# Attention and two expert layers on one core: a gather awaited on the load queue, more buffers for row statistics, and a new order of steps

## The chip, the cores and the metric

The kernel runs on one core of a Trainium2 chip. The metric is the device time of one execution in microseconds, as the median of several runs. The engines have short names in the profile: PE is TensorE (its matmuls; PEld is its loading of weights), DVE is VectorE, ACT is ScalarE, POOL is GpSimd, SP is SyncE, which here only issues transfers. Each engine carries out its own instructions in the order in which they are written, and waits for the others by semaphores.

## The reference

Three layers follow one another. The first is causal attention with 2 batches, 12 heads, 448 tokens and 64 columns a head:

```python
scores = scale * np.matmul(q, k.transpose(0, 1, 3, 2))      # scale = 1/8
scores = np.where(mask, -1000000000.0, scores)
scores = scores - np.max(scores, axis=-1, keepdims=True)
attn = np.exp(scores)
attn = attn / (np.sum(attn, axis=-1, keepdims=True) + 1e-09)
return np.matmul(attn, v).astype(np.float32)
```

Its output, 896 tokens of 768 columns, goes to a layer of 8 experts in which each token takes the expert with the largest logit (a cosine of token and expert embedding, over tau), `h = relu(x @ w1[e])`, `out = gate * (h @ w2[e])` with 1024 hidden columns and the softmax probability as the gate. Third, `h = max(max(x @ w1, x @ w2), x @ w3)` and `h @ w_out`, all 768 by 768, whose weights come in float64 and are decoded on the chip.

## The kernel before, in words

**Pairs.** Attention works on twelve pairs of heads, 0 to 9, a and b (hexadecimal); pairs 0 to 5 are batch 0, pairs 6 to b batch 1. The scores of a pair are cut into seven blocks of 64 queries (i = 0 to 6, with 64(i+1) keys), in four groups: {6}, {5, 0}, {4, 1}, {3, 2}. The order in which all this is issued is written out by hand in the strings of `SCHEDULE`, one word a step; `emit` reads the words one after the other, so a word's place is its place in the queue of each engine on which it works. A word begins with the pair; the next letter is the step:

- `L`, `V`: loads of K and Q, and of V, issued by SP. `q`: K times 1/8, by GpSimd (`2qp`), VectorE (`0qv`) or ScalarE (`6qs`), one instruction on 128x448.
- `S`, `Z`: TensorE's scores of a group's first and second block (a letter behind names the PSUM tag); `K`: the mask, added by a matmul.
- `M`: row maxima (VectorE); `E`: exponentials with row sums (ScalarE); `R`: reciprocal (VectorE). All three use the pair's tile `sm` (`sms[p]`), from a pool of two buffers.
- `N`: one block of `prb` is multiplied by the reciprocal, by VectorE, or with a `p` by GpSimd. `prb` has two buffers, for even and odd pairs.
- `T`: four transposes of `prb` (TensorE), `t`: their copy to `pt` by ScalarE (`s`) or VectorE (`v`). `T0` reads blocks 0 to 3, `T1` blocks 2 and 4 to 6, `T2` blocks 3 to 6, `T3` blocks 4 to 6.
- `A`: the product with V; `a`: its copy to `xt`. `X`: four transposes of `xt`, `x`: their copy to `x2T`, after which GpSimd stores the pair's columns into the DRAM tensor `xd`.

**Beside attention.** Words with `D` decode two weight units of the third layer early (`D10x` loads, `a`, none and `l` are stages). `EA`, `EM`, `ET` prepare the expert embeddings, whose rows lie in the tile `er`. `GA` to `G5` make the logits, `C0` and `C1` choose an expert for each token of a batch. `F1`, `F2`, `F3` (a chain of small VectorE instructions between matmuls) find the most frequent expert of batch 0 and up to 128 of its tokens. With that, slot 0 of the expert layer begins before attention is done: `L0` loads its four w1 tiles, `L1`, `L11` and `L13` its four w2 tiles (768 KB each, on SP; six buffers `raw` in turn), `W` words split them into a high part (ScalarE, `h`) and a low part (VectorE, `l`), `XG` gathers the 128 tokens from `xd` into `xrp` (an indirect transfer issued by GpSimd that must wait for the six stores of batch 0), `X0` and `X4` transpose them, and `H` words are its first layer.

**After attention.** The last string orders the routing of all tokens and slot 0's second layer (`P`, `Y`); then come up to 14 further slots of 128 tokens, and the third layer.

The functions that the diff touches, and what calls them:

Of the kernel before, what the change touches and what calls it, by code (L numbers as in the profile page):

```python
# [7 lines left out]
F32 = mybir.dt.float32  # L8
# [28 lines left out]
def kernel(  # L37
# [45 lines left out]
    xd = dram.tile([N, DM], F32, name="xd")  # L83

# [44 lines left out]
    def embed(tp):  # L129
        er = tp.tile([E, DM], F32, name="er")  # L130
        nc.scalar.dma_start(out=er, in_=emb)
        nc.scalar.dma_start(out=rtau, in_=tau.to_broadcast([P, 1]))
        sq = hp0[:E, :DM]
        es = tp.tile([E, 2], F32, name="es")
        table = tp.tile([E, 2], F32, name="table")
        nc.vector.memset(table, 1.0)
        nc.scalar.activation(out=table[:, 1:2], in_=table[:, 0:1], func=AF.Sqrt)
        return er, es, sq, table
# [282 lines left out]
    sm_p = att.enter_context(tc.tile_pool(name="sm", bufs=2))  # L421
# [297 lines left out]
    def reuse():  # L719
# [11 lines left out]
        "L0": lambda: wload0(0, (0, 1, 2, 3)), "L1": lambda: wload0(1, (0, 2)), "L11": lambda: wload0(1, (1,)), "L13": lambda: wload0(1, (3,)), "RE": reuse, "R0": lambda: held["S0"].relu(0),  # L731
# [429 lines left out]
```

## Time and profile before

| what | us |
|---|---|
| median of 3 runs | 474.25 |
| lowest and highest | 473.67, 474.72 |
| the profiled execution | 473.55 |
| its span in the profile | 471.8 |
| TensorE busy in it | 457.7 |
| VectorE busy | 323.2 |
| ScalarE busy | 266.9 |
| GpSimd busy | 81.0 |

The span is what the profiler saw from the program's first instruction to its last. Attention fills it up to about 106 us; from there to 300 us run the expert slots, then the third layer. A busy time is the union of an engine's instructions; waits inside it show only when the engine is looked at in order of time.

### The profile page before, as it was taken

What the parts mean: (1) busy time and instruction counts of PE and PEld (TensorE: products, weight loads), DVE (VectorE), ACT (ScalarE), POOL (GpSimd) and SP (SyncE); (2) the same over time, 40 slices, a digit from 0 to 9 for tenths busy, and PEclk for the clock granted to TensorE, in tenths of its full rate; (3) what the DMA queues carried; (4) which work ended last, traced back from release to release, by engine and by line L of the source; (5) the groups of instructions that cost most, each with busy time, mean ns of one, the idle gap of its engine ahead of it and who ended that gap; (6) DMA issues with size and microseconds to landing.
All of it is one profiled execution on the core that took longest, in us unless ns stands there. A gap on an engine that the chain in (4) does not pass through costs nothing. (4 is left out here: it accounts for less than half of the span.)

```text
span 471.8 us, 9239 instructions
## 1 busy us (share of the span) xinstructions
PE 457.7 (97%) x3158; PEld 405.8 (86%) x3158; DVE 323.2 (69%) x650; ACT 266.9 (57%) x560; POOL 81.0 (17%) x103
## 2 busy tenths in 40 slices
PE   8999999899999999999999999999999999999994
PEld 6787768688898998998999987989989989899993
DVE  5999999968454985110978955898989889840000
ACT  7898979867726896233988954544444353410000
POOL 4868474620010000000000000000000000001111
PEclk9999999999999999999999999999999999999998
DMA  8644229441158890119799903844534330000111
GB/s 272 251 124 163 65 76 408 183 130 51 34 171 320 309 354 21 35 38 350 279 320 370 365 24 131 343 141 142 180 140 144 125 135 1 1 0 35 67 68 67
DMA packets 18173, 75.85 MB, mean 161 GB/s; under 512 B 2360, under 2 KB 5432, under 8 KB 18112
## 3 DMA queue, kind: packets, MB, share of 16 engines
q1 hardware_dynamic: 15408, 65.05, 38.1%
q0 software_dynamic: 2400, 9.83, 5.6%
q8 instruction: 26, 0.43, 0.4%
q10 hardware_dynamic: 304, 0.25, 0.2%
q14 instruction: 35, 0.29, 0.2%
HBM read 69.62 MB, written 5.51 MB: 159 GB/s over the span
## 5 line engine op out<-in xcount | busy, mean ns | idle before, releaser
L975 PE MATMUL pm<-x2h,dwh 128*128 128x512 f32 (+1 forms) x204 | 74.1, 363 | 0.0
L976 PE MATMUL pm<-x2l,dwh 128*128 128x512 f32 (+1 forms) x204 | 74.0, 362 | 0.0
L977 PE MATMUL pm<-x2h,dwl 128*128 128x512 f32 (+1 forms) x204 | 74.0, 362 | 0.0
L981 PE MATMUL l<-w2h,hh 128*128 128x384 f32 x160 | 54.9, 343 | 0.7 <-ACT hh L207 0.7
L242 DVE TENSOR_TENSOR w1l<-raw,w1h 128x768 fp32r<-128x768 f32 x40 | 36.0, 950 | 27.8 <-PE l L981 20.5
L981 PE MATMUL l<-w2l,hh 128*128 128x384 f32 x160 | 53.7, 336 | 0.2 <-DVE w2l L262 0.2
L981 PE MATMUL l<-w1h,xhp 128*128 128x512 f32 x109 | 43.8, 402 | 0.0
L981 PE MATMUL l<-w1l,xhp 128*128 128x512 f32 x109 | 42.7, 391 | 0.0
L174 ACT CAST dwh<-dt_t 128x768 fp32r<-128x768 f32 (+1 forms) x20 | 15.5, 773 | 46.8 <-DVE dt_t L173 46.7
L977 PEld LDWEIGHTS pm<-x2h,dwl 128*128 128x128 f32 x204 | 38.3, 188 | 4.0
L975 PEld LDWEIGHTS pm<-x2h,dwh 128*128 128x128 f32 x204 | 38.3, 188 | 4.0
L976 PEld LDWEIGHTS pm<-x2l,dwh 128*128 128x128 f32 x204 | 38.3, 188 | 4.0
L517 ACT ACTIVATE prb<-pss,sm 128x64 f32<-128x64 f32 (+6 forms) x84 | 39.2, 492 | 3.3 <-DVE sm L510 2.2
L1115 POOL DMA_INDIRECT out_dram<-ob,sidx x7 | 6.9, 979 | 194.8 <-DVE ob L1114 194.8
L527 POOL TENSOR_SCALAR prb<-prb,sm 128x64 f32<-128x64 f32 (+6 forms) x38 | 36.0, 964 | 19.8 <-DVE sm L523 18.7
L198 POOL DMA_INDIRECT xrp<-xd,idx x11 | 11.3, 1029 | 153.0 <-PE xtp L216 143.1
L981 PE MATMUL l<-w2h,hl 128*128 128x384 f32 x160 | 36.3, 336 | 0.1
L242 DVE TENSOR_TENSOR w2l<-raw,w2h 128x768 fp32r<-128x768 f32 x40 | 35.1, 947 | 0.0
L204 DVE TENSOR_TENSOR hl<-htp,hh 128x512 fp32r<-128x512 f32 x17 | 11.7, 689 | 31.8 <-ACTq L351 17.8
L510 DVE TENSOR_REDUCE sm<-pss 128x1 f32<-128x128 f32 (+6 forms) x84 | 29.9, 412 | 2.9 <-PE pss L506 2.4
L241 ACT CAST w1h<-raw 128x768 fp32r<-128x768 f32 x40 | 31.7, 854 | 0.0
L981 PEld LDWEIGHTS l<-w2h,hh 128*128 128x128 f32 x160 | 30.0, 188 | 1.5 <-ACT hh L207 0.9
(255 smaller groups left out, 1022.4 us busy)
## 6 DMA issues: line engine op xcount, KB each, us to landing
raw<-in_moe_w_dram SPq DMA_DIRECT2D x48, 768.0 KB, 6.5
rawd<-in_moe_w_dram SPq DMA_DIRECT2D x18, 768.0 KB, 5.9
rawd<-in_moe_w_out_dram SPq DMA_DIRECT2D x6, 768.0 KB, 4.3
vr<-in_v_dram SPq DMA_DIRECT2D x12, 256.0 KB, 3.7
kt<-in_k_dram SPq DMA_DIRECT2D x12, 224.0 KB, 4.1
xd<-x2T POOLq DMA_DIRECT2D x12, 224.0 KB, 3.2
qt<-in_q_dram SPq DMA_DIRECT2D x11, 224.0 KB, 3.5
qt<-in_q_dram ACTq DMA_DIRECT2D x1, 224.0 KB
```

The costliest lines, as they stand in the source:

```text
L174: nc.scalar.copy(out=hi[:, c0:c1], in_=f)
L198: nc.gpsimd.indirect_dma_start(out=xrp, out_offset=None, in_=xd if i else xd[0:S], in_offset=bass.IndirectOffsetOnAxis(ap=idx[:, i:i + 1] ...
L204: nc.vector.tensor_tensor(out=lo, in0=ps_ap, in1=hi, op=ALU.subtract)
L241: nc.scalar.copy(out=hi[:, sl], in_=r[:, sl])
L242: nc.vector.tensor_tensor(out=lo[:, sl], in0=r[:, sl], in1=hi[:, sl], op=ALU.subtract)
L510: nc.vector.tensor_reduce(out=sms[p][:, 0, SC[i]:SC[i] + 1], in_=held["s", p, g][:, SO[i]:SO[i] + 64 * (i + 1)], axis=AX.X, op=ALU.max, ne ...
L517: nc.scalar.activation(out=prb[p % 2][:, poff[i]:poff[i] + n], in_=ps[:, SO[i]:SO[i] + n], func=AF.Exp, bias=sm[:, 0, SC[i]:SC[i] + 1], sc ...
L527: eng.tensor_scalar(out=r, in0=r, scalar1=sms[p][:, 2, SC[i]:SC[i] + 1], scalar2=None, op0=ALU.mult)
L975: nc.tensor.matmul(o, lhsT=lh, rhs=rh, start=first, stop=False)
L976: nc.tensor.matmul(o, lhsT=lh, rhs=rl, start=False, stop=False)
L977: nc.tensor.matmul(o, lhsT=ll, rhs=rh, start=False, stop=last)
L981: nc.tensor.matmul(o, lhsT=a, rhs=b, start=first and n == 0, stop=last and n == len(ops) - 1)
```

## The change

Four things are changed. The strings of `SCHEDULE` are written in a new order, with some steps on another engine: K's scaling leaves GpSimd (12 pairs: 9 by GpSimd and 3 by VectorE before, 8 by VectorE and 4 by ScalarE now), GpSimd has 43 normalisations where it had 38, and VectorE 41 for 46. A new word `LW`, ahead of `L1`, `L11` and `L13`, stores one number of `xrp` into a DRAM tensor `mark`, from SP's queue. The pool of `sm` has four buffers. The tile `er` is the first rows of `xrp`.

```diff
@@
+    mark = dram.tile([1, 1], F32, name="mark")
@@ def embed(tp):
-        er = tp.tile([E, DM], F32, name="er")
+        er = xrp[:E]
@@
-    sm_p = att.enter_context(tc.tile_pool(name="sm", bufs=2))
+    sm_p = att.enter_context(tc.tile_pool(name="sm", bufs=4))
@@ once = {
-        "L0": lambda: wload0(0, (0, 1, 2, 3)), "L1": lambda: wload0(1, (0, 2)), ...
+        "L0": lambda: wload0(0, (0, 1, 2, 3)), "LW": lambda: nc.sync.dma_start(out=mark, in_=xrp[0:1, 0:1]), "L1": lambda: wload0(1, (0, 2)), ...
@@ SCHEDULE (one of 14 strings; all are new)
-    "4X 9E0 8T0h 4xs 7A0a 7A2 7t2s 7A1 L0 aV 7A3 8t0s F2 bV 8N6p L1 9K3 6X 9K2 9E1 7as 9M2 5Xt bqp 6xs F3 5xv RE ..."
+    "4Xa C0 9M1 8N1p F1 7A0t 7A2 7A1 7A3 9S2h 4xs 9Z2 9K2 9E1 8N5p 8T0t 9E0 5Xa 7as 6Xa 8t0s F2 6xs 5xs L0 aV bV 9M2 F3 D11l RE ..."
```

One line is added above most of the code, so a line number of before is one higher after it. What moves is shown at three places.

SP's queue where the weights of slot 0 are loaded, before (`raw` is the buffer of a weight tile, `vr` that of V of pairs a and b):

```order
L236 DMA raw_1265<-in_moe_w1_dram 128x1536
L465 DMA vr2_163<-in_v_dram 128x512
L465 DMA vr3_164<-in_v_dram 128x512
L236 ISA
L236 DMA raw_1284<-in_moe_w2_dram 128x1536
L236 ISA
L236 DMA raw_1286<-in_moe_w2_dram 128x1536
```

and now:

```order
L237 DMA raw_1302<-in_moe_w1_dram 128x1536
L466 DMA vr2_164<-in_v_dram 128x512
L466 DMA vr3_165<-in_v_dram 128x512
L732 DMA mark_93<-xrp_85 1x1
L237 ISA
L237 DMA raw_1619<-in_moe_w2_dram 128x1536
L237 ISA
L237 DMA raw_1621<-in_moe_w2_dram 128x1536
```

The store into `mark`, which reads `xrp`, stands ahead of the w2 loads, which are unchanged among themselves.

GpSimd's queue around the gather into `xrp`, before (`prb1` is pair 9 up to the gather, `prb0` behind it is pair a; the stores are those of 4x, 6x and 5x):

```order
L594 DMA xd_92<-x2T0_120 112x4x128
L527 TENSOR_SCALAR prb0_150<-prb0_150,sm_877 128x448
L481 TENSOR_SCALAR kt_1042<-kt_1042 128x448
L594 DMA xd_92<-x2T1_121 112x4x128
L594 DMA xd_92<-x2T0_120 112x4x128
L527 TENSOR_SCALAR prb1_151<-prb1_151,sm_1092 128x64
L527 TENSOR_SCALAR prb1_151<-prb1_151,sm_1092 128x128
L527 TENSOR_SCALAR prb1_151<-prb1_151,sm_1092 128x384
L198 DMA xrp_85<-xd_92,idx0_110 128x768
L527 TENSOR_SCALAR prb0_150<-prb0_150,sm_1359 128x128
L527 TENSOR_SCALAR prb0_150<-prb0_150,sm_1359 128x192
L527 TENSOR_SCALAR prb0_150<-prb0_150,sm_1359 128x64
```

and now (`prb1` is pair 9, `prb0` pair 8 above the gather and pair a below it; the last `prb1` is pair b):

```order
L528 TENSOR_SCALAR prb0_151<-prb0_151,sm_987 128x384
L595 DMA xd_92<-x2T1_122 112x4x128
L595 DMA xd_92<-x2T0_121 112x4x128
L528 TENSOR_SCALAR prb1_152<-prb1_152,sm_1045 128x256
L528 TENSOR_SCALAR prb1_152<-prb1_152,sm_1045 128x192
L199 DMA xrp_85<-xd_92,idx0_111 128x768
L528 TENSOR_SCALAR prb1_152<-prb1_152,sm_1045 128x320
L528 TENSOR_SCALAR prb0_151<-prb0_151,sm_1356 128x128
L528 TENSOR_SCALAR prb0_151<-prb0_151,sm_1356 128x192
L528 TENSOR_SCALAR prb0_151<-prb0_151,sm_1356 128x256
L528 TENSOR_SCALAR prb0_151<-prb0_151,sm_1356 128x64
L528 TENSOR_SCALAR prb0_151<-prb0_151,sm_1356 128x384
```

A scaling of K no longer stands between the stores, and behind the gather stands first a normalisation of pair 9 (320 columns, block 4), which VectorE did before.

VectorE's queue at the start, before (`kt` is K of a pair, `sm` a pair's row statistics, `pss` its scores):

```order
L479 TENSOR_SCALAR kt_171<-kt_171 128x448
L479 TENSOR_SCALAR kt_231<-kt_231 128x448
L510 TENSOR_REDUCE sm_246<-pss_247 128x1
L510 TENSOR_REDUCE sm_246<-pss_251 128x1 x2
L510 TENSOR_REDUCE sm_246<-pss_266 128x1 x2
L510 TENSOR_REDUCE sm_259<-pss_260 128x1
L510 TENSOR_REDUCE sm_246<-pss_283 128x1 x2
L510 TENSOR_REDUCE sm_259<-pss_296 128x1 x2
L510 TENSOR_REDUCE sm_259<-pss_280 128x1 x2
```

and now:

```order
L480 TENSOR_SCALAR kt_172<-kt_172 128x448
L511 TENSOR_REDUCE sm_245<-pss_246 128x1
L480 TENSOR_SCALAR kt_231<-kt_231 128x448
L511 TENSOR_REDUCE sm_245<-pss_261 128x1 x2
L511 TENSOR_REDUCE sm_245<-pss_249 128x1 x2
L511 TENSOR_REDUCE sm_245<-pss_257 128x1 x2
L480 TENSOR_SCALAR kt_235<-kt_235 128x448
L511 TENSOR_REDUCE sm_293<-pss_294 128x1
L511 TENSOR_REDUCE sm_293<-pss_302 128x1 x2
```

The scaling of pair 2's K has come in between the row maxima, and the maxima of pair 0 are done before those of pair 1 begin.

## Rows read from the trace of the kernel before

**Rows 1.** stretch, us, then busy us (instructions) of PE, PEld, DVE, ACT, POOL

```profile
5.00:64.80 59.80, 58.02 (x742) 43.27 (x739) 56.08 (x157) 53.31 (x176) 38.91 (x38) 1.00 0.50 164
70.50:105.70 35.20, 33.62 (x358) 27.80 (x359) 30.57 (x68) 28.23 (x71) 15.96 (x19) 1.00 0.64 244
...
120.00:300.00 180.00, 179.15 (x1007) 162.52 (x1006) 108.13 (x175) 114.78 (x194) 9.95 (x13) 1.00 0.58 216
```

**Rows 2.** TensorE in order of time: start, us, line, tiles, count, [idle before it]

```profile
64.85 0.25 PE L653 MATMUL cnt<-oh,ones 112*128 112x8 bf16 x4
...
70.46 0.45 PE L697 MATMUL ix<-pay,A 112*128 112x1 bf16 x8 [0.73 <-DVE pay L91]
70.78 1.51 PE L537 MATMUL pst<-ident,prb 128*128 128x128 f32 x12
72.21 1.15 PE L500 MATMUL pss<-kt,qt 64*64 64x448 f32 x12
...
78.54 0.37 PE L506 MATMUL pss<-maskb,identb 128*128 128x64 bf16 x7
...
82.52 0.65 PE L588 MATMUL psm<-ident,xt 128*112 128x128 f32 x4
84.31 0.66 PE L537 MATMUL pst<-ident,prb 128*128 128x128 f32 x4 [1.14 <-POOL prb L527]
85.36 1.09 PE L537 MATMUL pst<-ident,prb 128*128 128x128 f32 x8 [0.40 <-POOL prb L527]
...
87.38 0.84 PE L216 MATMUL xtp<-ident,xrp 128*128 128x128 f32 x6
```

**Rows 3.** GpSimd in order of time, around the gather of slot 0

```profile
71.34 1.59 POOL L594 DMA_DIRECT2D xd<-x2T  x2 [0.19 <-issue]
...
81.31 1.09 POOL L198 DMA_INDIRECT xrp<-xd,idx  x1 [3.37 <-DVE sm L510]
82.44 2.87 POOL L527 TENSOR_SCALAR prb<-prb,sm 128x128 f32<-128x128 f32 x4
```

**Rows 4.** stores into xd issued from 71 to 73 us, the tile's view

```profile
DMA to landing us min/median/max: 7.6/7.9/8.2
```

**Rows 5.** transfers into raw issued from 67 to 73 us: first and last start

```profile
L236 SPq DMA_DIRECT2D raw<-in_moe_w_dram x6: 332/347/827, 67.7 to 72.4; - x6
```

**Rows 6.** the store into xd issued at 67.4 us

```profile
DMA to landing us min/median/max: 5.6/5.6/5.6
```

**Rows 7.** the gather into xrp issued at 81.3 us

```profile
DMA to landing us min/median/max: 5.9/5.9/5.9
```

**Rows 8.** the two gathers into xrp issued from 100 to 130 us

```profile
DMA to landing us min/median/max: 3.7/3.8/3.9
```

**Rows 9.** groups until F1, by shape: busy us, mean ns, idle before, releasers

```profile
L481 POOL TENSOR_SCALAR kt<-kt 128x448 f32<-128x448 f32 x8 | 11.7, 1471 | 3.2 <-DMA kt<-in_k_dram 3.2
...
L527 POOL TENSOR_SCALAR prb<-prb,sm 128x320 f32<-128x320 f32 x6 | 6.9, 1150 | 0.7 <-DVE sm L523 0.7
...
L527 DVE TENSOR_SCALAR prb<-prb,sm 128x384 f32<-128x384 f32 x6 | 4.2, 705 | 0.0
...
L473 DVE COPY pt<-pst 128x512 f32<-128x512 f32 x3 | 2.0, 679 | 0.0
...
L479 DVE TENSOR_SCALAR kt<-kt 128x448 f32<-128x448 f32 x3 | 1.5, 487 | 2.6 <-DMA kt<-in_k_dram 2.6
...
L527 DVE TENSOR_SCALAR prb<-prb,sm 128x320 f32<-128x320 f32 x3 | 1.1, 376 | 0.0
```

**Rows 10.** ScalarE in order of time, from 66 to 93 us

```profile
70.44 0.61 ACT L475 COPY x2T<-psm 112x512 f32<-112x512 f32 x1
...
91.63 1.59 ACT L260 CAST w2h<-raw 128x768 fp32r<-128x768 f32 x2
```

**Rows 11.** the weight transfer into raw issued at 95.5 us

```profile
DMA to landing us min/median/max: 4.8/4.8/4.8
```

**Rows 12.** VectorE in order of time, after C1

```profile
109.53 0.69 DVE L91 TENSOR_TENSOR A<-i,jj 112x512 bf16<-112x512 f32 x1
```

More of the change, by code (lines that the diff above doesn't have):

```diff
@@ L730 @@
         "X0h": lambda: split_hi(held["X0"]), "X0l": lambda: split_lo(held["X0"]), "X4h": lambda: split_hi(held["X4"]), "X4l": lambda: split_lo(held["X4"]),
-        "L0": lambda: wload0(0, (0, 1, 2, 3)), "L1": lambda: wload0(1, (0, 2)), "L11": lambda: wload0(1, (1,)), "L13": lambda: wload0(1, (3,)), "RE": reuse, "R0": lambda: held["S0"].relu(0),
+        "L0": lambda: wload0(0, (0, 1, 2, 3)), "LW": lambda: nc.sync.dma_start(out=mark, in_=xrp[0:1, 0:1]), "L1": lambda: wload0(1, (0, 2)), "L11": lambda: wload0(1, (1,)), "L13": lambda: wload0(1, (3,)), "RE": reuse, "R0": lambda: held["S0"].relu(0),
     }
```

28 rows, old and new, of the table SCHEDULE are left out of this document.

## The prediction

> **What bounds the kernel now.** I read the busy table by stretch first [rows 1]. TensorE is busy 179.15 of 180 us between 120 and 300 us, and none of the change's code runs there: the later steps keep their order and simply follow when the earlier ones end. The change lives in the attention part, which on TensorE runs from about 5 to 105.7 us. There TensorE is busy 58.02 of 59.80 us and 33.62 of 35.20 us, but VectorE is nearly as full: 56.08 of 59.80 us and 30.57 of 35.20 us, ScalarE 53.31 and 28.23 us. So three engines are close to full there, and TensorE can gain only what it now waits, a few us of 474. What follows F1 is one long chain of TensorE instructions, so a wait removed there reaches the end, unless VectorE becomes the later one.
>
> Next I read TensorE in order of time from F1 (64.85 us) on [rows 2], for gaps between a row's start and the next one's. Twelve transposes at 70.78 us take until 72.21 us, 0.119 us each. From 82.52 to 87.38 us stand 24 such transposes (7X, aT0, aT3, aT1, 9X, aT2); at that rate they need 2.86 us and take 4.86 us. So **2.0 us** are lost here, and two rows say to whom: 1.14 and 0.40 us on GpSimd's normalisations. GpSimd's own rows give the cause [rows 3]: it sat 3.37 us before the gather of slot 0 at 81.31 us, and the four normalisations that aT0 and aT3 read are behind the gather in its queue. The view names a row maximum as the releaser, long done; the gather reads what six stores write, and the last of these was issued just after 72 us and took 8.2 us to land [rows 4], so about 80.4 us, 0.9 us before the gather starts. Those stores lasted so long because four w1 transfers, two of V and two of w2, 5 MB together, had been issued around them, the six of weights from 67.7 to 72.4 us [rows 5]; an earlier store, issued just ahead of w1, took 5.6 us [rows 6]. The gather itself took 5.9 us [rows 7], two later ones with quiet queues 3.7 and 3.9 us [rows 8].
>
> **Part A: the await (LW), and GpSimd's queue around the gather.** LW is a 4-byte store that reads a gathered word, so SP stops there until the gather has landed; behind it on SP are only the four w2 transfers (and slot 1's loads after them). The two w2 transfers that now go out at about 71.4 us go out after the gather instead, so 1.5 MB less are moving under the stores and the gather. But the order also moves a normalisation (9N4p, 320 columns) behind the gather on GpSimd, and 9T2 waits for it. I work that out from F3 (70.46 us) as zero [rows 2]: now TensorE goes from F3 through 8T, the scores of pairs a and b, 8A and one step of 9T until 78.54 us; the same steps stand between F3 and 9T2 in the new order, so it comes to 9T2 after 8.1 us. On GpSimd the way from the last store's landing to the end of 9N4p is 0.9 us to the gather's start, 1.1 us for its issue (81.31 to 82.44) [rows 3] and 1.15 us for 320 columns [rows 9], 3.2 us. The store of 5X is issued 1.7 us after F3 now, since its copy waits behind others. After the change 6X and 5X are copied by ScalarE directly behind one another; their transposes I put some 4.1 us after F1 (7A, a group of 9's scores, 8T's first step and themselves, at the rates of [rows 2]), two copies of 0.6 us [rows 10] and one store issue of 0.8 us later the second store goes out, near 0.2 us before F3 (F3 is 5.6 us after F1). Landing takes 5.6 us (w1 alone ahead) to 8.2 us (as now). The wait at 9T2 is then -0.2 + 5.6 + 3.2 - 8.1 = 0.5 us at the least, 3.1 us with the slow landing, and 5.0 us if the store goes out no earlier either. I take a landing of 6.3 us, nearer to the row without w2: 1.2 us in place of 2.0. **A = -0.8 us, bounds -1.5 and +3.0.**
>
> The gather's landing falls too, but buys little: X0 now starts at 87.38 us, behind the transposes that were late themselves. What LW delays: w2 would land some 5 us (4.8 us for one transfer, [rows 11]) after a gather that lands about F3 + 12 us, so by about F3 + 18. The first split of w2 on ScalarE runs now at 91.63 us, F3 + 21 [rows 10], ahead of H00; in the new order it stands behind H05, so F3 + 19 is early for it. LW's own price is hidden under these us; if the gather lands more than some 2 us late, each further us holds up ScalarE and then TensorE.
>
> On the DMA queues the Trainium skill (DMA: Bandwidth & Descriptors, "Queues, rings and completion order") says that each DMA engine goes round the queues it has work for, packet by packet. By that rule w2, behind w1 in SP's queue, takes nothing from GpSimd's until w1 is through, and the sum is the third rival's, +0.3 us in place of -1.6. The gather's 5.9 us against 3.7 to 3.9 show that other traffic does cost it 2 us; of the stores no row says which traffic it was.
>
> **Part B: K's eighth, normalisations and copies until F1.** Until F1, GpSimd loses 8 scalings of K at 1.47 us [rows 9], 11.8 us, and gets 6 more normalisations (32 for 26). VectorE gets 5 scalings (0.49 us each, +2.4), 2 more pt copies (+1.4), one x copy less (-0.7), and one tail of a decode goes behind F1 (-0.6). Of normalisations it has by width: 384 columns five less (at 0.705 us, -3.5), 192, 256 and 448 one less each (-1.35 together, taken at 0.45), 320 three more (at 0.376, +1.1). Sum: -1.25 us of VectorE time. ScalarE gets 4 scalings and an x copy, and loses one pt copy: +2 us of 6.5 free. As VectorE had 3.7 us free in 59.8, its work is what TensorE follows until F1, and I count 1.0 us of it. The bound: 384 columns took 0.705 us on average while a tile of 320 took 0.376, so some of the 3.5 us was waiting and not work; at 0.45 us the sum is zero. In the other direction the free time that TensorE still had, 1.8 us, could go as well. **B = -1.0 us, bounds +1.0 (an order that fits worse) and -2.5.**
>
> **Part C: four buffers of row statistics, er in xrp.** With two, a row maximum of pair p+2 waited for the last normalisation of pair p. In front of VectorE's row maxima no long wait stands in this stretch (3.7 us idle in all, [rows 1]); the new order uses the freedom, the buffers alone give 0. Bounds -0.5 and 0. The tile er lies in xrp until the gather writes it, 60 us later: 0.
>
> **Part D: after C1.** One of the one-hot halves (A0, 0.69 us [rows 12]) goes ahead of P0's low half on VectorE, and two 0.2 us operations behind it; TensorE's first steps of layer 2 wait for it. **+0.2 us**, bounds -0.2 and +0.6.
>
> **The sum.** -0.8 - 1.0 + 0 + 0.2 = -1.6 us. The profiled execution took 473.55 us (span 471.8, the rest around it), the median is 474.25; the former would give 471.95, on the median I forecast **472.6 us**. Its own range, with A from -1.5 to 0 and B from -2.5 to 0, is 470.2 to 473.3.
>
> **The rivals.**
> First, **slower**: the wait moves to 9T2. If the stores land as late as now (8.2 us) and the second goes out only 0.6 us earlier (F3 + 1.1), 9T2 waits 1.1 + 8.2 + 3.2 - 8.1 = 4.4 us, 2.4 more than is lost now; with B at 0 and D that is 474.25 + 2.6 = 476.8, with B at -1.0 it is 475.8. It decides from a landing later than F3 + 6.9 us: there the wait equals the 2.0 us lost now. For it: w1 alone is 3 MB of the 5. Against it: the 5.6 us row. Time 475.8.
> Second, **no change**: the scalings on VectorE wait for GpSimd. That 384 columns take VectorE 0.705 us and 320 take 0.376 says that some of them stood still, by about 0.3 us on the mean. GpSimd has 32 long instructions until F1 where it had 34, and VectorE 38 tensor_scalars of this kind in both, so the same waits fall on others: the five scalings cost 0.3 us more each, and the five 384s bring only 0.4 each. B is -1.25 + 1.5 + 1.5 = +1.75 us at the worst, about +0.3 us halfway, and the time 474.25 - 0.8 + 0.3 + 0.2 = 474.0. The Trainium skill (SBUF — State Buffer, "Who interferes with whom") states such a rule: a VectorE tensor_scalar from SBUF and a GpSimd instruction can shut each other out for a whole instruction. The two rows agree with it, as far as they go.
> Third, **the await does nothing**: by turns between the queues w2 never delayed the stores. Then landing stays at 8.2 us, only the earlier issue counts: 3.1 us for 2.0, A = +1.1, and with B and D 474.25 + 0.3 = 474.6.
>
> **How the numbers follow.** About 0.2% (0.95 us) is what a measurement of this kernel can tell from no change: faster is below 473.3, slower above 475.2. Forecast 0.54, first rival 0.22, second 0.14, third 0.10. Of the forecast 0.50 lies below 473.3 and 0.04 above; of the second 0.04 and of the third 0.02 fall below, and 0.02 of the third above 475.2. That makes faster 0.56, same 0.20, slower 0.24. The range from 470.2 to 475.9 takes in the forecast's own range, the two rivals without change, and the slower one up to its middle; 0.11 above and 0.07 below are left out.
>
> **What would show it.** In the profile after: (1) the stores of batch 0 land 5.6 to 6.5 us after issue, the gather in about 3.8, and the w2 transfers are issued after it; if the stores still take 8 us, A's first step was wrong. (2) TensorE waits about 1 us at 9T2, and no longer at aT0 and aT3; 3 us or more is the first rival. (3) F1 begins about 1 us earlier than 64.85 us; if not, B fell. (4) ScalarE doesn't wait for w2 at its first split. A time below 470 would mean that TensorE's small waits before F1, which I left at what they are, went away too; one above 476 that SP's stop made w2 late.

## The result and the profile after

The changed kernel took 478.1 us (median of 8 runs, 477.26 to 480.37) against 474.49 us for the kernel before, measured beside it (8 runs, 473.34 to 476.45): a ratio of 1.0078, 95% interval 1.0052 to 1.0104. It is slower by 0.8%, above the forecast of 472.6 us and above the upper end of its range, 475.9 us. The profiled execution took 477.6 us, its span 475.9.

The stretches of [rows 1] look like this in the kernel after (stretch, its length, busy us and instructions of PE, PEld, DVE, ACT, POOL, granted clock, DMA share, GB/s):

```profile
5.00:64.80 59.80, 58.67 (x746) 44.96 (x745) 54.36 (x157) 54.65 (x178) 34.11 (x35) 1.00 0.48 165
70.50:105.70 35.20, 30.16 (x313) 25.05 (x313) 26.49 (x59) 26.65 (x67) 13.91 (x17) 0.95 0.64 228
120.00:300.00 180.00, 179.15 (x1010) 162.55 (x1009) 105.73 (x172) 115.67 (x197) 10.01 (x13) 1.00 0.57 207
```

Up to F1 VectorE is 1.7 us less busy than before, as forecast, and from 120 us on nothing changed. In between TensorE lost 3.5 us of work in the same 35.2 us, and the granted clock is 0.95 where it was 1.00. Where, TensorE's order of time tells, beside [rows 2]:

```profile
64.85 0.24 PE L654 MATMUL cnt<-oh,ones 112*128 112x8 bf16 x4
...
68.58 1.04 PE L589 MATMUL psm<-ident,xt 128*112 128x128 f32 x8
69.70 0.45 PE L698 MATMUL ix<-pay,A 112*128 112x1 bf16 x8
70.02 1.51 PE L538 MATMUL pst<-ident,prb 128*128 128x128 f32 x12
...
77.23 0.74 PE L538 MATMUL pst<-ident,prb 128*128 128x128 f32 x5
83.02 2.61 PE L538 MATMUL pst<-ident,prb 128*128 128x128 f32 x11 [5.04 <-POOL prb L528]
85.42 0.86 PE L589 MATMUL psm<-ident,xt 128*112 128x128 f32 x4
86.22 1.98 PE L579 MATMUL psa<-pt,vr 128*64 128x128 f32 x32
...
109.82 0.19 PE L646 MATMUL rk<-oh,upper 112*112 112x64 bf16 x1
```

One wait of **5.04 us** stands at 83.02 us. The five transposes ahead of it are 9T0 and the first of 9T2; the next of 9T2 reads what 9N4p writes. GpSimd's rows, beside [rows 3], say why it is late:

```profile
66.69 0.74 POOL L595 DMA_DIRECT2D xd<-x2T  x1 [0.53 <-ACT x2T L476]
...
70.53 1.45 POOL L595 DMA_DIRECT2D xd<-x2T  x2 [1.81 <-ACT x2T L476]
73.35 1.79 POOL L528 TENSOR_SCALAR prb<-prb,sm 128x256 f32<-128x256 f32 x2 [1.37 <-DVE sm L524]
80.45 1.36 POOL L199 DMA_INDIRECT xrp<-xd,idx  x1 [5.32 <-DVE prb L528]
81.85 4.95 POOL L528 TENSOR_SCALAR prb<-prb,sm 128x320 f32<-128x320 f32 x6
```

GpSimd stood 5.32 us before the gather, and six normalisations stand behind it, 9N4p first (81.85 to 82.97). As in [rows 3], the releaser that the view names had long been done; the gather needed the last of pair 5's store. The stores and the gather landed so (the two stores issued from 70 to 73 us, the one at 66.7 us, the gather at 80.45 us), beside [rows 4, 6, 7]:

```profile
DMA to landing us min/median/max: 7.6/7.9/8.3
```

```profile
DMA to landing us min/median/max: 2.8/2.8/2.8
```

```profile
DMA to landing us min/median/max: 4.2/4.2/4.2
```

w2's transfers do go out behind the gather now (85.31 us and later), and the two stores landed as late as ever: 7.6 and 8.3 us, where it was 7.6 and 8.2. Behind the wait the clock is low:

```profile
82.00:84.00 2.00, 0.98 (x5) 0.98 (x6) 0.00 (x0) 0.04 (x1) 2.00 (x3) 0.63 0.70 187
84.00:86.00 2.00, 2.00 (x11) 2.00 (x10) 0.00 (x0) 1.46 (x3) 2.00 (x4) 0.51 0.06 17
```

0.51 is the 1.2 GHz level. The 15 transposes from 83.02 to 86.22 us took 3.20 us; at the 0.119 us each of [rows 2] they are 1.79, so the low clock cost 1.4 us.

From F3 to the first matmul of the rank (rk above, 105.68 us in the kernel before) it is 40.12 us now and was 35.22: +4.90. TensorE's idle time there went from 1.58 to 5.04 us (+3.46), and the clock took 1.4. That is all of it.

### The profile page after: what moved, and what is told of

Read it like the earlier page. It is cut to its first block, busy times and chain, and to the rows that moved or that the text cites. A ratio compares the mean times of both kernels' runs of the same rounds, so it can differ in the third digit from the quotient of the medians.

```text
span 475.9 us, 9224 instructions
## 1 busy us (share of the span) xinstructions
PE 459.7 (97%) x3158; PEld 408.7 (86%) x3158; DVE 319.8 (67%) x651; ACT 268.4 (56%) x563; POOL 74.8 (16%) x99
## 3 DMA queue, kind: packets, MB, share of 16 engines
HBM read 69.62 MB, written 5.51 MB: 158 GB/s over the span
## 5 line engine op out<-in xcount | busy, mean ns | idle before, releaser
L528 POOL TENSOR_SCALAR prb<-prb,sm 128x384 f32<-128x384 f32 (+6 forms) x43 | 42.1, 999 | 25.5 <-ACT prb L518 8.9
L511 DVE TENSOR_REDUCE sm<-pss 128x1 f32<-128x448 f32 (+6 forms) x84 | 30.2, 412 | 4.1 <-PE pss L507 4.1
L538 PE MATMUL pst<-ident,prb 128*128 128x128 f32 x192 | 26.8, 286 | 6.1 <-POOL prb L528 6.1
L242 ACT CAST w2h<-raw 128x768 fp32r<-128x768 f32 x40 | 30.5, 842 | 2.3 <-SPq L352 1.5
```

What stands on the lines that cost most here:

```text
L242: nc.scalar.copy(out=hi[:, sl], in_=r[:, sl])
L511: nc.vector.tensor_reduce(out=sms[p][:, 0, SC[i]:SC[i] + 1], in_=held["s", p, g][:, SO[i]:SO[i] + 64 * (i + 1)], axis=AX.X, op=ALU.max, ne ...
L528: eng.tensor_scalar(out=r, in0=r, scalar1=sms[p][:, 2, SC[i]:SC[i] + 1], scalar2=None, op0=ALU.mult)
L538: nc.tensor.transpose(ps[:, n * P:(n + 1) * P], prb[p % 2][:, poff[i] + kt * P:poff[i] + (kt + 1) * P], ident)
```

## The experiments

Fifteen more kernels were measured. All are edits of one of the two kernels, so four marks on TensorE compare them: the first transposes of pair 0 (about 13 or 14 us; they start late in some executions of either order), F1, F3 and the rank's first matmul. Behind the latter the kernels do not differ. Of the strings of `SCHEDULE` the diffs below show only the words around an edit. All in us, from the profiled executions; the time is the median of the runs, the ratio is to the kernel before on the same chip:

| kernel | pair 0 to F1 | F1 to F3 | F3 to rank | idle in it | time | ratio, 95% interval |
|---|---|---|---|---|---|---|
| before | 51.59 | 5.61 | 35.22 | 1.58 | 474.49 | |
| after | 50.68 | 4.85 | 40.12 | 5.04 | 478.1 | 1.0078 [1.0052, 1.0104] |
| a1 gather behind 9N4p | 50.71 | 4.60 | 37.27 | 2.22 | 472.19 | 0.9954 [0.9938, 0.9971] |
| a2 without the await | 50.67 | 4.66 | 41.78 | 5.69 | 478.13 | 1.0087 [1.0060, 1.0113] |
| a3 w1 split | 50.71 | 4.60 | 39.25 | 4.27 | 477.26 | 1.0058 [1.0039, 1.0076] |
| c1 filler | 50.69 | 4.60 | 38.74 | 0.63 | 475.97 | 1.0040 [1.0022, 1.0057] |
| a5 gather behind aN2p | 50.69 | 4.60 | 34.84 | 1.19 | 471.68 | 0.9936 [0.9915, 0.9957] |
| a6 gather behind aN0p | 50.68 | 4.65 | 35.83 | 1.78 | 472.97 | 0.9982 [0.9967, 0.9996] |
| a12 a5 without the await | 50.73 | 4.61 | 36.21 | 2.29 | 473.9 | 1.0018 [0.9992, 1.0045] |
| a10 store early | 50.70 | 5.97 | 34.03 | 0.48 | 473.5 | 0.9980 [0.9963, 0.9996] |
| a11 store early, gather behind 9N4p | 50.70 | 4.89 | 33.43 | 0.00 | 471.86 | 0.9944 [0.9928, 0.9959] |
| a9 K's eighth on GpSimd | 59.35 | 5.35 | 40.24 | 5.17 | 487.14 | 1.0292 [1.0255, 1.0330] |
| b1 before + await | 51.55 | 5.61 | 36.01 | 2.36 | 475.13 | 1.0020 [1.0010, 1.0029] |
| b3 before + gather behind aN2p | 51.55 | 5.61 | 35.26 | 1.63 | 474.32 | 1.0002 [0.9991, 1.0012] |
| b4 before + both of these | 51.55 | 5.61 | 35.38 | 1.72 | 474.99 | 1.0024 [1.0005, 1.0042] |
| b5 before + store early | 51.57 | 6.42 | 34.12 | 1.08 | 474.54 | 1.0008 [0.9994, 1.0022] |
| b2 before + buffers | 50.99 | 5.57 | 35.30 | 1.66 | 473.57 | 0.9988 [0.9979, 0.9998] |

The idle time of c1 leaves out its 4.63 us of filler.

### a1: the gather behind 9N4p

```diff
-8A1 XG 8av aE0
+8A1 8av aE0
...
-bZ2 9N4p bS1
+bZ2 9N4p XG bS1
```

> The kernel after with slot 0's gather issued behind 9N4p on GpSimd instead of ahead of it. Theory (TensorE's 5.0 us at 83.0 come from 9N4p standing behind a gather that waits for its two stores, and the drop of the clock to 0.51-0.63 behind it comes from that idle time): no wait of more than 0.5 us at 9T2, no granted clock under 0.9 between 78 and 88 us, GC's own stall stays, and at most the 2 us by which the rows of before waited for GpSimd's normalisations of pair a; 478.1 - 5.0 - 1.4, and 0 to 2 given back: 471.7 to 474. Rival (the new order of steps leaves TensorE short of work there anyway, the gather is only the last of several late things): a wait of 3 us or more returns within 5 us of the old place, 476.5 to 478.5.

472.19 us, 5.9 less than the kernel after, by an edit of one place in GpSimd's queue: the theory. TensorE in order of time, and the stretch from 84 to 88 us (the granted clock is the third number from the end):

```profile
84.37 1.11 PE L538 MATMUL pst<-ident,prb 128*128 128x128 f32 x4 [2.22 <-POOL prb L528]
```

```profile
84.00:88.00 4.00, 3.63 (x19) 3.63 (x20) 0.17 (x2) 0.78 (x2) 2.58 (x3) 0.57 0.64 209
```

The wait at 9T2 is gone. One of 2.22 us came at aT0, whose four normalisations are still behind the gather: a little over the 2 us that were the upper bound of what was expected to come back. That the clock would fall behind 2.22 us too, I had not expected.

### a2: without the await

```diff
-H00 H01 LW bT0t
+H00 H01 bT0t
```

> The kernel after without the one-element store that waits for the gather, so that w2's six transfers are again issued behind w1's (the first two at once). Theory (what delays the stores is w1's four transfers and V's two, which stand ahead of them in both kernels; w2 behind them delays nothing but the gather's own landing): the second store lands 8.0 to 8.6 us after its issue as in the kernel after (8.3), the gather 5.5 to 6.2 us after its own (4.2 with the await), TensorE's wait at 9T2 stays at 4.7 to 5.4 us; 477.3 to 479. Rival (the prediction's Part A, the await keeps 1.3 to 2 us off the stores): the second store lands over 9.3 us after its issue and the wait at 9T2 grows by as much, 479.3 to 480.5.

478.13 us: the await makes no difference to the time of the kernel after. The landing of the two stores, then TensorE's wait:

```profile
DMA to landing us min/median/max: 8.1/8.6/9.1
```

```profile
82.77 2.61 PE L538 MATMUL pst<-ident,prb 128*128 128x128 f32 x11 [5.69 <-POOL prb L528]
```

The second store took 9.05 us where it took 8.30. But it scatters: in the kernels that are alike up to that store and have the await (after, a1, c1, a5, a6) it took 8.30, 7.69, 8.39, 8.89 and 8.47 us (and 9.22 in a9), and in a12, the other one without the await, 8.24. So no cost of w2, behind w1 in SP's queue, is shown for the stores, and nothing like the 1.9 us that Part A put on it. The gather landed in 5.2 us, with the await in 4.2; nothing waited for that here.

### b1: the await alone, in the kernel before

```diff
-8N6p L1 9K3
+8N6p 9K3
...
-8A1 XG 8A3
+8A1 XG LW L1 8A3
```

(and the two lines of the change that define `mark` and `LW`)

> The kernel before with the await alone: the one-element store behind the gather in SP's queue, and the first two transfers of w2 behind it, nothing else changed. Theory: stores 7.6 to 8.3 us after their issue as before, gather 3.8 to 4.4 instead of 5.9, w2 landed some 10 to 15 us later without a wait of ScalarE for it, time 474.5 within 0.7. Rival, Part A of the prediction: second store 6.3 us, GpSimd free 1.9 us earlier, the 2.0 us that TensorE lost behind 82.5 gone, 472.5 to 473.2.

475.13 us, a little slower. The second store landed in 7.87 us (8.21 before, 8.07 in b3 and 8.36 in b2, which both lack the await), the gather in 3.90 (5.93). TensorE gained 0.3 us at the old place and met a new wait, with its cause on ScalarE (first TensorE's, then ScalarE's order of time):

```profile
95.42 0.65 PE L589 MATMUL psm<-ident,xt 128*112 128x128 f32 x4 [1.11 <-ACT x2T L476]
```

```profile
94.05 0.83 ACT L261 CAST w2h<-raw 128x768 fp32r<-128x768 f32 x1 [1.43 <-DMA raw<-in_moe_w_dram]
```

So the await has a price in the old order: ScalarE waits 1.43 us for a w2 that came late, and its copy behind that holds TensorE. The theory had expected no such wait. In the kernel after, whose order splits w2 later, ScalarE waits nowhere for it.

### a3: half of w1 behind the await

```diff
-"L0": lambda: wload0(0, (0, 1, 2, 3)), ...
+"L0": lambda: wload0(0, (0, 1)), "L02": lambda: wload0(0, (2, 3)), ...
...
-H00 H01 LW bT0t
+H00 H01 LW L02 bT0t
```

> The kernel after with only two of w1's four transfers ahead of the stores; the other two go behind the await, ahead of w2's. Theory (the stores land when the bytes that stood before them are through; 1.5 MB less): the second store 5 to 6.5 us after its issue instead of 8.3, TensorE's wait at 9T2 2 to 3 us shorter (2 to 3 us left), a smaller drop of the clock; 474.7 to 476.2. Rival (the landing is set by the store itself, its 112 rows or what lies on GpSimd's queue): 7.6 to 8.3 as before, 5 us at 9T2, 477.5 to 478.7. A wait for the later w1 or w2 transfers on ScalarE behind 92 us would add to either.

The stores landed in 6.97 and 6.74 us. The last one came 1.6 us sooner than in the kernel after with 1.5 MB less of w1 ahead of it, and 1.0 to 2.2 us sooner than in the five kernels listed under a2; the first (6.94 to 7.90 there) hardly. So w1 is a part of what stood in the last store's way; what the other 6.7 us are was not tried. The wait shrank by 0.77 us only:

```profile
81.06 2.61 PE L538 MATMUL pst<-ident,prb 128*128 128x128 f32 x11 [4.27 <-POOL prb L528]
```

9N4p itself took 1.92 us in this run (79.08 to 81.00) where it took 1.11, and ate half of the gain. Beside it VectorE made the low half of a w1 tile (`w1l`, from two tiles in SBUF):

```profile
79.08 1.92 POOL L528 TENSOR_SCALAR prb<-prb,sm 128x320 f32<-128x320 f32 x1
79.12 0.94 DVE L263 TENSOR_TENSOR w1l<-raw,w1h 128x768 fp32r<-128x768 f32 x1
```

In the kernel after `w1l` had ended before 9N4p began. The last section has more such pairs. The mechanism is as expected, the size missed: 477.26 us for 474.7 to 476.2, not clearly below the 478.1 of the kernel after.

### c1: TensorE kept busy during the wait

```diff
         ps = held["t", p, g] = bank(tag, "pst", BUFS[tag])
+        if (p, g) == (9, 2):
+            for n in range(80):
+                nc.tensor.matmul(ps[:, :P], lhsT=identb, rhs=identb, start=True, stop=True)
```

> The kernel after with 80 matmuls of ident's 16-bit copy with itself (128x128, results overwritten) ahead of 9T2's transposes, so that TensorE is busy for most of its 5.0 us wait; GpSimd's work unchanged. Theory (the transposes after the wait are slow because the granted clock fell to its 1.2 GHz level behind the idle time): the wait ends where it ended, F3 + 13.3, the granted clock between 82 and 86 is over 0.9 instead of 0.51 to 0.63, the 15 transposes behind the wait take 1.8 us instead of 3.2; 476.3 to 477.2. Rival (they are slow because the normalisations feed them one by one): 3.2 us again, 477.6 to 478.6.

475.97 us, about 2 less than the kernel after and a little under the expected 476.3, with nothing else moved; the intervals of the two ratios just overlap. The wait ended 13.37 us behind F3 (13.32 in the kernel after), as TensorE's order of time and the stretch behind it show:

```profile
81.56 1.42 PE L541 MATMUL pst<-ident,prb 128*128 128x128 f32 x11 [0.63 <-POOL prb L528]
82.81 0.60 PE L592 MATMUL psm<-ident,xt 128*112 128x128 f32 x4
83.34 1.98 PE L582 MATMUL psa<-pt,vr 128*64 128x128 f32 x32
```

```profile
82.00:84.00 2.00, 2.00 (x23) 1.79 (x23) 0.00 (x0) 1.86 (x4) 2.00 (x4) 1.00 0.18 74
```

The same 15 transposes take 1.78 us instead of 3.20 at a clock of 1.00. So the low clock is a cost of its own, 1.4 us in the trace; what the median shows beyond that is not located.

### a5, a6: the gather behind two and behind four normalisations of pair a

```diff
-8A1 XG 8av aE0
+8A1 8av aE0
...
-9T2b aN2p bM2
+9T2b aN2p XG bM2
```

a6 has it behind aN0p instead, and the first four transposes of the gathered rows (X0) behind aT1 and aT2:

```diff
-bE0 aN0p bE2
+bE0 aN0p XG bE2
...
-bN0 X0 X0h bN4p aT1t aT2 GS1
+bN0 bN4p aT1t aT2 X0 X0h GS1
```

> The kernel after with the gather behind 9N4p, aN1p and aN2p on GpSimd (it stood behind 9N4p alone in the run that gave 472.19). Theory (what is left there, 2.2 us at aT0 and a clock of 0.57 behind it, is again normalisations behind the gather, now aN1p to aN0p; pair a's reciprocal is there at 77.6 and the stores land at 78.2, so two of the four fit ahead of the gather for nothing): the wait at aT0 is 0.7 us or less, the granted clock stays over 0.9, 469.8 to 471.2. Rival (TensorE then meets the gathered rows themselves, whose transposes stand 0.8 us behind aT0): the wait moves to the transposes of xrp, 1 to 2 us, 471.5 to 472.5.

> The kernel after with the gather behind all four normalisations that aT0 needs (aN1p, aN2p, aN3p, aN0p) and the four transposes of the gathered rows behind aT1 and aT2. Theory: no wait over 0.5 us at aT0, the gather issued at 81 to 82 and landed at 85 to 86, the transposes of xrp at 84.5 to 85 wait up to 1 us for it; 469.8 to 471.5. Rival (the landing now decides): 1.5 to 2.5 us of waiting at the transposes of xrp, clock down behind it, 471.5 to 473.

a5 gave 471.68 us, the lowest median, though a1 and a11 cannot be told from it, and a little above its expected range: 1.19 us left at aT0, no drop of the clock behind them (1.00 from 84 to 86 us), the gather landed in 3.9 us and nobody waited for it. a6 gave 472.97: no wait at aT0, but 1.32 us at aT1, because aN5p now stood behind the gather and took 2.08 us instead of 1.23, beside a `w1l` as 9N4p in a3. The time is in the rival's range, but neither theory nor rival had named that wait. Each of the places tried in GpSimd's queue has its own victim.

### b3, b4: the same late gather in the kernel before

b3 moves XG behind aN2p there; b4 also adds the await behind it, with L1, as in b1.

```diff
-8A1 XG 8A3
+8A1 8A3
...
-8Xa aN2p 9t1s
+8Xa aN2p XG 9t1s
```

> The kernel before with its gather behind aN1p and aN2p on GpSimd, nothing else changed. Theory (the 2.0 us lost at 82.5 to 87.4 in the kernel before have the same cause, normalisations behind a gather that waits for its stores): its waits of 1.14 and 0.40 us go or shrink to under 0.5 in sum, 472.4 to 473.4. Rival (there the reciprocal of pair a, which comes at 79.3 and two VectorE steps later than in the kernel after, sets the wait): 473.7 to 474.5. The difference to the 472.19 of the kernel after with its gather behind 9N4p is what the other parts of the change are worth.

> The kernel before with the gather behind aN1p and aN2p and with the await (w2's first two transfers behind it): the two edits of which each alone gave nothing there. Theory: the gather lands 3.8 to 4.4 us after its issue instead of 5.8, the 1.29 us at the transposes of its rows go, 472.6 to 473.4. Rival (w2 then lands late enough to be waited for, as the 1.11 us at 95.4 in the run with the await alone, or the time is bound elsewhere): 474 to 475.2.

Both theories fell: 474.32 and 474.99 us. What waits in b3, and in b4:

```profile
87.56 0.85 PE L216 MATMUL xtp<-ident,xrp 128*128 128x128 f32 x6 [1.29 <-DMA xrp<-xd,idx]
```

```profile
95.58 0.65 PE L589 MATMUL psm<-ident,xt 128*112 128x128 f32 x4 [1.38 <-ACT x2T L476]
```

In b3 the waits of [rows 2] shrank from 1.54 to 0.28 us, and 1.29 came at the gathered rows, which landed 5.8 us after the issue. In b4 the landing took 3.9 us and that wait was gone, and ScalarE's wait for w2 took its place, as in b1. In the kernel before, the 2.0 us could not be had by GpSimd's queue, nor by the await, nor by both: each of three limits hides the next, with a wait of 1.3 to 1.5 us.

### a12: a5 without the await

```diff
-H00 H01 LW bT0t
+H00 H01 bT0t
```

> The kernel after with the gather behind 9N4p, aN1p and aN2p, as in the run that gave 471.68, but without the await. Theory (the await is worth what it takes off the gather's own landing, once the gather stands late enough to be waited for itself): the gather lands 5.2 to 6 us after its issue instead of 3.9, the transposes of its rows wait 0.8 to 1.8 us, 472.4 to 473.6. Rival (the await is worth nothing in any order): 471.2 to 472.2.

473.9 us against 471.68 with the await, a little above the theory's range. TensorE's wait for the gathered rows, and the gather's landing:

```profile
86.41 0.63 PE L217 MATMUL xtp<-ident,xrp 128*128 128x128 f32 x4 [1.85 <-DMA xrp<-xd,idx]
```

```profile
DMA to landing us min/median/max: 5.9/5.9/5.9
```

From F3 to the rank it is 36.21 us for 34.84. So the await is worth something after all, by the gather's own landing (3.9 for 5.9 us), once the gather stands so late that its rows are waited for: 1.4 us in the traces, 2.2 in the medians. With the early gather (a2) it is worth nothing.

### a10, a11, b5: the last store earlier

a10 puts 5X behind F1, in the tag `a` that it had, and its copy behind 4X's; b5 does the same in the kernel before, with 5X behind 4X. a11 is a1 with 5X in PSUM tag t (7A's in b), so that it needn't wait for 4X's copy. This is a11's edit, beside that of a1:

```diff
-F1 7A0t 7A2 7A1 7A3 9S2h 4xs 9Z2
+F1 5Xt 7A0b 7A2 7A1 7A3 9S2h 4xs 5xs 9Z2
...
-8T0t 9E0 5Xa 7as 6Xa
+8T0t 9E0 7as 6Xa
...
-F2 6xs 5xs L0
+F2 6xs L0
```

> The kernel after with pair 5's transposes to rows (5X) right behind F1, and its copy and store behind pair 4's, ahead of pair 6's; the gather stays where the change put it, ahead of 9N4p. Theory (the wait's first cause is that the last store the gather needs is issued 1.6 us behind F3, behind w1's four transfers; the store ahead of it, issued at 66.7, landed in 2.8 us): the store lands before 74, the gather is issued as soon as 9N2p ends, no wait at 9T2, at most 0.5 us at aT0, F3 to the rank matmul 33.5 to 34.5 us instead of 40.1; 469.3 to 471. Rival (another thing stands right behind: pair a's reciprocal at 77.5 and four normalisations, or the store lands as late as ever among w1's packets): 1 to 2 us of waiting at aT0 or 9T2, 471 to 473.

> The kernel before with the same edit alone: 5X behind 4X, its copy on ScalarE and its store behind pair 4's. Theory (the 2.0 us that the kernel before loses at 82.5 to 87.4 come from the gather's wait for that store): the gather issued by 79, the waits of 1.14 and 0.40 us gone, F3 to the rank matmul 33.6 to 34.3 us instead of 35.2; 472.3 to 473.3. Rival (they come from pair a's reciprocal at 79.3 and the row of normalisations behind it): 473.7 to 474.6.

> The kernel after with 5X behind F1 in another PSUM tag (t, and 7A in tag b, so that it does not wait for 4X's copy as it did for 1.16 us in the run before), its copy and store behind pair 4's, and the gather behind 9N4p. Theory (late store and early gather are the whole of the loss, the rest of the change is worth 1.5 to 2 us): F1 to F3 4.6 to 4.9 us, F3 to the rank matmul 33.5 to 34.3, no wait over 0.5 us between F3 and the rank matmul; 470 to 471.3. Rival (the earlier transposes and the earlier store cost elsewhere what they give, as in the run before): 472 to 473.5.

a10: the gather went out at 77.17 us, the wait fell to 0.48 us, and F3 to the rank took 34.03 us, as the theory has it. But 5X waited 1.16 us for a PSUM bank right behind F1 and pushed F3, so that 473.5 us were left, above both expectations. b5: F3 to the rank 1.1 us shorter, F1 to F3 0.8 us longer, time the same; pair a's normalisations were no longer waited for, but the gathered rows, which landed in 8.0 us, for 0.94 us. a11 has neither wait (the stretch from F3 to the rank, and GpSimd's row of the gather):

```profile
69.59:103.03 33.44, 33.44 (x358) 28.05 (x359) 29.87 (x69) 28.05 (x70) 14.43 (x17) 1.00 0.67 255
```

```profile
76.26 1.15 POOL L199 DMA_INDIRECT xrp<-xd,idx  x1 [0.18 <-issue]
```

From F3 to the rank TensorE is busy all 33.44 us at full clock. 471.86 us is a little above the expected 470 to 471.3, and 6.2 under the kernel after. So in this stretch the late store and the early gather are the whole of the loss; with both mended the change is worth 2.3 us against the kernel before. Either alone gives back most of it: 472.19 us in a1, 473.5 in a10.

### a9: K's eighth back on GpSimd

```diff
-2qv
+2qp
...
-bqs
+bqp
```

(the same for pairs 3 to 8 and a)

> The kernel after with the scalings of K by an eighth on GpSimd again for the nine pairs that had them there in the kernel before, at their new places in the order; nothing else changed. Theory of the prediction's Part B (VectorE's and GpSimd's load until F1 is what the change lightens, 1.0 us at F1): F1 0.5 to 1.0 us later than in the kernel after, 478.4 to 479.3. Rival (TensorE's own work and the order of steps set F1, the scalings lie beside it on either engine): F1 within 0.3, 477.6 to 478.5.

487.14 us. The way to F1 is 8.7 us longer, far over both expectations. TensorE now waits for GpSimd, for a scaled K and twice for normalisations:

```profile
39.11 1.72 PE L501 MATMUL pss<-kt,qt 64*64 64x448 f32 x14 [2.79 <-POOL kt L482]
...
55.34 0.66 PE L538 MATMUL pst<-ident,prb 128*128 128x128 f32 x4 [1.61 <-POOL prb L528]
56.83 0.87 PE L538 MATMUL pst<-ident,prb 128*128 128x128 f32 x3 [0.84 <-POOL prb L528]
```

The clock fell twice on the way as well (0.50 from 40 to 42 and from 58 to 60 us): up to F1 TensorE idles 6.6 us where it idled 1.1, and its work takes 61.01 us for 58.67. Nine scalings of 1.37 us in the queue ahead of normalisations that the new order needs soon are not hidden: at these places the new order needs K's eighth off GpSimd.

### b2: the buffers alone, in the kernel before

```diff
-        er = tp.tile([E, DM], F32, name="er")
+        er = xrp[:E]
...
-    sm_p = att.enter_context(tc.tile_pool(name="sm", bufs=2))
+    sm_p = att.enter_context(tc.tile_pool(name="sm", bufs=4))
```

> The kernel before with four buffers for row maxima instead of two and the expert table loaded into the gathered rows' tile, and nothing else of the change. Theory (Part C: no engine waits for such a buffer in the old order): the same, 474.3 within 0.6, F1 and F3 within 0.3 us. Rival (row maxima of a pair wait for the buffer of two pairs before): 0.5 to 1.5 us earlier at F1, 472.8 to 473.8.

473.57 us, 0.8 less than the kernel before, and the way to F1 0.6 us shorter: the rival by its smaller end. No single wait shows it.

## Why the prediction was wrong, point by point

**What bounds the kernel** held: TensorE from 120 us on is unchanged, and each us lost or won between F1 and the rank came through to the end (366.0 to 366.2 us behind the rank, but for the three executions named in the last section). That the 2.0 us at 82.5 to 87.4 were GpSimd's queue and no more was too simple: b3 and b4 show two further limits directly behind.

**Part A is the step that failed.** It said -0.8 and the stretch gave +4.9. Its equation for the wait at 9T2 was right: with what was measured it is 1.57 (the second store's issue behind F3) + 8.30 (landing) + 3.40 (landing to the end of 9N4p) - 8.28 (TensorE's arrival) = 5.0 us, and 5.04 were seen. Two of its terms were mis-sized, and they make the 3.8 us by which the wait missed the forecast of 1.2.
The landing, put at 6.3, was 8.30 us. I took the row without w2 [rows 6] for the nearer one, but that store was issued just ahead of w1, the later one behind all of it. a3 shows that w1 stood in the way (some 1.6 us for half of it); no run shows that w2 did. The right neighbour was the 8.2 of [rows 4].
The issue, put at F3 - 0.2, was F3 + 1.57: the store went out 1.0 us later behind F1 than worked out (6.4 us for 5.4), and F3 itself came 0.8 us nearer. The terms that the prediction names, 4.1 + 1.2 + 0.8 us, make 6.1 and not 5.4, so most of the 1.0 us was there to be seen. What the trace adds: the transposes ended 4.8 us behind F1 (69.62 us) and not 4.1, and the copies waited for them, not for the copy of 8T0 ahead of them:

```profile
69.65 1.07 ACT L476 COPY x2T<-psm 112x512 f32<-112x512 f32 x2 [0.23 <-PE psm L589]
```

And the sum had no term for the clock, which c1 shows as a cost of its own: 1.4 us in the trace, about 2 in the median.

On the DMA queues the third rival's rule held for the stores, as far as these runs can tell: the Trainium skill (DMA: Bandwidth & Descriptors, "Queues, rings and completion order") has each DMA engine go round the queues that have work, packet by packet. By that rule w2, second in SP's own queue, should not matter to GpSimd's stores, and the traces agree: without the await the second store took 8.24 and 9.05 us in the new order and 8.07 to 8.36 in the old, with it 7.69 to 9.22 and 7.87 to 8.24. What no store showed, the gather did: 5.2 to 8.0 us in the six kernels without the await, 3.8 to 4.6 in those with it, but for a10 and a11. Their gathers went out at 77.17 and 76.26 us, 4.3 and 6.3 us before V's last transfer had landed, and took 5.2 and 6.1.

**LW's own price**, called hidden, was hidden in the kernel after, but b1 and b4 show 1.1 to 1.4 us in the old order. A time above 476 us was to mean that SP's stop made w2 late; that isn't what made this one. Its use was not where Part A looked for it: not in the stores, but in the gather's landing, 2.2 us in the median of a12 against a5 and 1.4 in their traces.

**Part B** (-1.0 at F1) was right in size. F1 stands at 64.85 us in both traces, but the execution of the kernel after began late: its first transposes start at 14.16 us for 13.26. From there to F1 it is 50.68 instead of 51.59, and 50.67 to 50.73 in the nine other kernels with that order up to F1: -0.9. F1 to F3 gave another -0.8 to -1.0 that no part had forecast. Of its reason a9 shows the half that the prediction didn't count: the new order needs GpSimd's relief. VectorE's share was not tried by itself. With the -0.1 of Part D the stretches add up to +3.1 us; the medians differ by 3.6, and the rest is not located.

**Part C** at nothing was wrong by a little: b2 gives -0.6 us up to F1, so that this much of B's -0.9 may be C's. **Part D** (+0.2) was within its bounds: from the rank to the end 366.17 us before, 366.07 after.

**The range and the rivals.** The forecast's own range doesn't follow from the bounds named for it: A from -1.5 to 0 and B from -2.5 to 0 with D's 0.2 give 470.45 to 474.45 us, not 470.2 to 473.3. The result lies outside either. The first rival, the wait at 9T2, is what happened: place and cause as written and its condition nearly (the second store went out at F3 + 1.57 where it has 1.1), 4.4 us of waiting forecast and 5.04 seen. Its 475.8 us lacked the clock. The second, VectorE slowed by GpSimd, did not show: VectorE is busy 54.36 us up to F1 where it was 56.08. (The reverse, GpSimd slowed beside VectorE, is seen around the gather; see the last section.) The third was right on its cause, as far as the runs tell (none shows that w2 delayed the stores), and wrong on the result, since it kept the early issue. The chance of 0.22 for the first rival was too low: its only counterargument was [rows 6].

## What to carry to other kernels

An instruction that waits for a landing holds all that stands behind it in its engine's queue (5.32 us on GpSimd here): before one is moved or put under a wait, list what stands behind it and when that is needed, and give the landing the price of the row with the same bytes in flight ahead of it, not of the cheapest row. A wait that is taken away pays only down to the next limit, so edits that give nothing alone (the await, the later gather, the earlier store) can be worth 2 us together, in another order of steps. And a wait on TensorE can be paid twice, the second time in the clock behind it (1.4 us behind 5.04 us here).

## What the runs showed of the hardware

The granted clock fell to its lower level behind idle stretches of 5.69 us (a2, 0.50), 5.04 us (0.51), 4.27 us (a3, 0.54), 2.79 us (a9, 0.50) and 2.22 us (a1, 0.55 to 0.60 for 4 us), and behind 1.61 us with 0.84 close behind it (a9, 0.50). The three other runs of a1 were 1.4 to 1.8 us shorter than the traced one, at mean clocks of 0.996 to 0.998 for its 0.994, so there it seems not to have fallen each time. It did not fall behind 1.85 us in the trace of a12, behind 1.19 us in a5, nor behind the 1.14 and 0.40 us of [rows 2].

How long a store of 224 KB takes to land depends steeply on when it is issued beside w1's four transfers: 2.8 us for one issued 1.0 us ahead of the first of them (after), 5.6 and 6.2 us for those issued 0.3 us ahead (before, a11), 8.2 us for one 0.3 us behind it (a10), and 8.3 us for one 3.5 us behind it (after).

GpSimd's instructions around the gather take longer where VectorE makes a `w1l` beside them. With all of its 0.94 us beside them normalisations took 1.92 us for 320 columns (a3) and 2.08 and 2.06 for 384 (a6, a12), where 1.11 and 1.23 are the rule; with 0.69 us of it beside them, 1.48 us for 256 columns (a1, a6, a10, a11; 0.98 in the kernel after); and the issue of the gather, 1.08 us in most kernels, took 1.82 in a1 with 0.87 us of it and 1.36 in the kernel after with 0.41. Where `w1l` began in the last 0.25 to 0.45 us of a normalisation, that one lost nothing (before, a11). That `w1l` is the cause is read from these overlaps; no run takes it away.

The stretch behind the rank, 366.0 to 366.2 us in most executions, took 367.7 to 367.8 in those of a3, a5 and a11, where TensorE falls behind bit by bit until some 290 us and no further; why is not known. So single executions are compared by stretches here and kernels by their medians.
